# Pooled attention and a token/channel MLP on one core: scalings ahead of loads, heads that meet V sooner, and copies shared out anew

## The chip, the core and the metric

The kernel runs on one core of a Trainium2 chip. A core has five engines that work side by side, each with its own instruction stream: TensorE for matmuls (PE in the profile; its weight loads are listed as PEld), VectorE (DVE), ScalarE (ACT), GpSimd (POOL) and SyncE (SP), which here only issues transfers. POOL and ACT issue transfers too; the transfers themselves (DMA) run on the core's 16 DMA engines. [...] The metric is the device time of one execution in microseconds (us), as a median over runs.

## The reference

For each of 8 batches: attention with 8 heads of 64 columns over 576 tokens, with K and V averaged over groups of 8 tokens (72 groups), and behind it one block of a ResMLP, which mixes tokens and then channels. Cut to what matters:

```
k_p = k.reshape(B, H, 72, 8, D).mean(axis=3)
v_p = v.reshape(B, H, 72, 8, D).mean(axis=3)
scores = q @ k_p.T / sqrt(64)
attn = softmax(scores)
x = (attn @ v_p)                      # heads side by side: (B, 576, 512)
a1 = alpha1 * x + beta1
tok = einsum('ts,bsd->btd', w_tok, a1)
u = x + lam * tok
a2 = alpha2 * u + beta2
ch = relu(a2 @ w_ch1) @ w_ch2         # 512 -> 2048 -> 512
out = u + lam * ch
```

## The kernel before, in words

Matmul operands are in bf16 or f16, sums in f32. The batches are gone through in order. Attention of a batch gives x_tm, its x with the tokens in the partitions (4 chunks of 128, and a rest of 64 that two batches share a chunk for); the token mix turns it into u; u is transposed, and the MLP works on blocks of 4 such chunks (512 tokens). While PE does the MLP of one block it also does the attention and the mix of the next batch in between, and the order of all this is written by hand; no scheduler decides anything. The steps of one batch, as the change touches them:

- `att_F` (L591) transposes q on PE, L598 copies it out. `scores` and `scores_rest` (L707, L726 in the first batch; `att_S4`, L759 and L764, later) are the matmuls of q with the pooled K. ACT takes their exponentials (L712, L731, later L780) into ET.
- `first_V` (L685, copied out by L687) pools V for the first batch on PE. Later batches sum V on DVE: `att_V` (L697) adds halves of the 8 tokens of a group three times; the last one writes vp, the pooled V of four heads.
- `att_AV` (L798, L802) multiplies ET of one head with vp. A column of ones in vp gives the sum of the exponentials too. Then DVE takes its reciprocal (L805) and writes the product into x_tm (L807).
- `att_X` (L821) and `rest_X` (L814) scale x_tm of two or more heads by lam times alpha1 into xs, on POOL or DVE. The vector lam times alpha1 is spread over the partitions at the start in two halves by `spread_lamal` (PE L496, copied by L499).
- `mix_T` does the token mix (L887, w_tok transposed against xs), adds x_tm (L894, u_sb) and casts the sum to bf16 (L898, u_bf). In the first batch it goes by two column halves, one with heads 0 to 3 and one with heads 4 to 7. The 65th row of the weights holds row sums (`setup_rowsum`, L529 and L532), for beta1.
- `mix_uT` transposes u_bf. In the first block PE does it (L912), and the copy out of PSUM (L919 on ACT, four chunks of 128x128; or L922 on DVE, one instruction of 128x512) multiplies by alpha2.
- `mlp_A` is the first channel matmul (L944) with L952 (ACT, relu and bias, into H); `mlp_B` is the second (L965). In the first block a call of `mlp_A` does half the tokens and an extra column that gives the bias (L948).

The first batch has almost nothing to lie beside, and its order is the string `order` in the function at the end. Each word names a generator in `plan`, and each mention of a word runs that generator to its next `yield`; so the first `A2` is PE's matmuls of head 2 and the second is the reciprocal and the product on DVE. The letters: A is `att_AV` of a head, X and R are `att_X` and `rest_X`, F the q transposes, Q and P scores and exponentials, V `first_V`, s `spread_lamal`, W and r the transposes of w_tok (L516, copied by L520) and row sums, M `mix_T`, T `mix_uT`, H and G the two token halves of `mlp_A`. Loads stand in the same string: k0 and k1 (L301) are the two halves of K of the next batch, l1 to l4 the weights of the MLP (L557, L563), va and vb V of the next batch (L308). All of these are issued by POOL, in the order of the string and among POOL's own work; lr (L321) is issued by SP.

For later batches `attention(b)` makes a list of steps, each with a due time, and they are sorted by it and put among the matmuls of the MLP. A due time sets only the place in each engine's stream.

Of the kernel before, what the change touches and what calls it, by code (L numbers as in the profile page):

```python
# [10 lines left out]
AF = mybir.ActivationFunctionType  # L11
ALU = mybir.AluOpType
AX = mybir.AxisListType

P = 128
# [195 lines left out]
def kernel(  # L211
# [18 lines left out]
    nc = tc.nc  # L230
# [11 lines left out]
    def gp(name):  # L242
        if pair[0]:
            return psB.tile([P, 512], FP, tag="ch", bufs=2, name=name)
        return psA.tile([P, 512], FP, tag="gp", name=name)

    def whole(parts):
        for _ in parts:
            pass
# [150 lines left out]
    early = const.tile([P, 2, DM], F16, tag="early", name="early")  # L400
# [90 lines left out]
    def spread_lamal(half, copy):  # L491

        ps = gp("ps_bc")[:, 0:256]
        cols = slice(256 * half, 256 * half + 256)
        for c in range(2):
            nc.tensor.matmul(out=ps[:, 128 * c:128 * c + 128], lhsT=pick[:, 2 * half + c],  # L496
                             rhs=part)
        yield
        copy(out=lamal_bc[:, cols], in_=ps)  # L499
# [50 lines left out]
    al2_cols = const.tile([P, 4], FP, tag="al2_cols", name="al2_cols")  # L550
# [127 lines left out]
    def first_V(u, copy):  # L678

        ps_v = gp("ps_v")  # L680
        vp = ps_v[0:SPG, 0:4 * D]
        heads = slice(4 * u, 4 * u + 4)
        terms = [(identity_bf[0:SPG, 0:SPG], st1[0]["v16"][:, heads, c]) for c in range(8)]
        for i, (weights, t) in enumerate(terms):
            nc.tensor.matmul(out=vp, lhsT=weights, rhs=t, start=(i == 0), stop=(i == len(terms) - 1))  # L685
        yield
        copy(out=vp1_pool[u][:, :, 0:64], in_=vp.rearrange("p (h d) -> p h d", h=4))  # L687
# [212 lines left out]
    def mix_uT(key, copy=None):  # L900
        s = st2[key]
        i = where[key]
        blk, at = i // 4, i % 4
        if blk not in u_fm:
            u_fm[blk] = work.tile([P, 4, 512], BF, tag="u_fm", bufs=3, name="u_fm")
        if blk:
            nc.sync.dma_start_transpose(out=u_fm[blk][:, :, 128 * at:128 * at + 128],
                                        in_=s["u_bf"])
            return
        ps_uT = gp("ps_uT").bitcast(BF)  # L910
        for cc in range(4):
            nc.tensor.transpose(out=ps_uT[0:P, 128 * cc:128 * cc + 128],  # L912
                                in_=s["u_bf"][:, 128 * cc:128 * cc + 128], identity=identity_bf)
        yield
        o = u_fm[blk][:, :, at // 2, 128 * (at % 2):128 * (at % 2) + 128]
        i = ps_uT[:, 0:512].rearrange("p (c t) -> p c t", t=128)
        if copy is scalar:
            for cc in range(4):
                nc.scalar.activation(out=o[:, cc], in_=i[:, cc], func=AF.Copy, bias=0.0,  # L919
                                     scale=al2_cols[:, cc:cc + 1])  # L920
        else:
            nc.vector.tensor_tensor(out=o, in0=i, in1=al2_cols.unsqueeze(2).to_broadcast((P, 4, P)),  # L922
                                    op=ALU.mult)


    H4 = {}
# [292 lines left out]
    vector, scalar = nc.vector.tensor_copy, nc.scalar.copy  # L1219
# [18 lines left out]
        plan[f"K{u}"] = att_K(0, u, copy)  # L1238
    for u, copy in enumerate((vector, vector)):
        plan[f"V{u}"] = first_V(u, copy)  # L1240
    for u, copy in enumerate((vector, scalar)):
        plan[f"s{u}"] = spread_lamal(u, copy)
    for i, copy in enumerate((scalar, vector, scalar, vector)):
        plan[f"F{i}"], plan[f"P{i}"] = att_F(0, i, copy), scores(i)
# [5 lines left out]
        plan[f"R{h}"] = once(lambda h=h, n=n, eng=eng: rest_X(0, h, h + n, eng))  # L1250
    for c, copy in enumerate((vector, scalar, scalar, scalar, scalar)):
        plan[f"W{c}"] = setup_wtok(c, copy)
    for c, copies in enumerate(((scalar, scalar), (scalar, vector), (vector, vector), (vector, scalar))):
        plan[f"r{c}"] = setup_rowsum(c)
        plan[f"M{c}"], plan[f"T{c}"] = mix_T(0, c, copies[0]), mix_uT((0, c), copies[1])
        plan[f"H{c}"], plan[f"G{c}"] = mlp_A(0, c, 0, 256), mlp_A(0, c, 256, 512)
    in_pair = "A0 A3 F2 K0 M1 P1 T1 T3 W0 r0 r1 s0 s1".split()
    order = (
# [6 lines left out]
    for name in order.split():  # L1265
# [5 lines left out]
    def attention(b):  # L1271


        first = b == 1
        todo = []
        if first:
            for hp in range(4):
                todo.append((2.6 + 0.9 * hp, lambda hp=hp: whole(att_F(b, hp))))
            todo.append((3.5, lambda: cast_rem(b, nc.gpsimd, behind=nc.vector)))
            for u in range(2):  # L1280
                todo.append((3.65 + 0.1 * u, lambda u=u: load_w2(2 + u)))
            todo.append((7.4, lambda: whole(att_Frem(b, nc.scalar.copy))))
        if b < B - 1:
            at = 28.5 if first else 10.0
            todo.append((at, lambda: whole(att_F(b + 1, 0))))
            todo.append((at + 0.1, lambda: whole(att_F(b + 1, 2))))
            todo.append((19.3 if first else 23.1, lambda: cast_rem(
                b + 1, nc.gpsimd, behind=None if first else nc.vector)))
            todo.append((26.72 if b > 1 else 27.2, lambda: whole(att_Frem(b + 1))))
        for u in range(2):  # L1290
            if first:
                todo.append((3.6 + 0.1 * u, lambda u=u: sum_k(b, u, nc.gpsimd)))
            if b > 1:
                on_act = u == 0 or b == 3
                todo.append((2.5 + 2.0 * u if on_act else 8.55, lambda u=u, on_act=on_act:
                             add_rest(b, u, nc.scalar.copy if on_act else None)))
            if 1 < b < B - 1:
                todo.append((26.5 + 0.1 * u, lambda u=u: sum_k(b + 1, u, nc.gpsimd)))
                todo.append((26.73 + 0.1 * u, lambda u=u: turn_k(b + 1, u)))
            if b > 2:  # L1300
                todo.append(((4.1, 8.95)[u], lambda u=u: pool_k(b, u)))
                continue
            if first:
                todo.append((19.1 + 0.1 * u, lambda u=u: sum_k(2, u, nc.gpsimd)))
            todo.append((7.0 + 2.3 * u if first else 2.9 + 2.0 * u,
                         lambda u=u: whole(
                             att_K(b, u, nc.vector.tensor_copy if first else nc.scalar.copy))))
        for u in range(2):
            at = (9.0 if first else 6.3, 14.05 if first else 13.6)[u]
            todo.append((at, lambda u=u: att_S4(b, u)))  # L1310
            for k, dt in enumerate((0.1, 0.1, 0.1, 0.7, 1.7, 1.75) if u else ((0.1, 0.1, 0.1, 1.1, 2.1, 2.95) if first else (0.1, 0.1, 0.95, 1.0, 2.1, 3.1))):
                todo.append((at + dt, lambda u=u, k=k: st1[b]["exp", u](k)))
            early = (5.2, 5.7, 3.7, 4.2) if first else (5.7, 6.2, 2.9, 3.6)
            for i, dt in enumerate((2.9, 3.4, 4.6, 5.1) if u else early):
                h = 4 * u + i
                todo.append((at + dt, lambda h=h: whole(att_AV(b, h))))
                if i % 2:
                    eng = nc.gpsimd if h == 5 or first and h < 5 else nc.vector
                    todo.append((at + dt + 0.1, lambda h=h, eng=eng: att_X(b, h - 1, h + 1, eng)))
        for u in range(2):  # L1320
            when = (0.2, 1.4, 2.2), (12.7, 12.8, 13.0) if b == 2 else (5.0, 7.2, 8.0)
            if first:
                when = (10.6, 10.7, 10.8), (12.5, 14.3, 14.4)
            for i, at in enumerate(when[u]):
                todo.append((at, lambda u=u, i=i: att_V(b, u, 4 >> i)))
        for c in range(5):
            at = 22.0 + 1.1 * c if first else 21.0 + (1.3 if b == 2 else 1.15) * c
            if c < 4 or b % 2:
                todo.append((at, lambda c=c: whole(mix_T(b, c))))
                key = (b, c) if c < 4 else (b - 1, 4)  # L1330
                todo.append((at + 1.8, lambda key=key: whole(mix_uT(key))))
        return todo
# [22 lines left out]
    for n in range(NBLK):  # L1355
# [42 lines left out]
        if n >= FIRST:  # L1398
            when = ((3, (4.6, 14.6)), (1, (8.6, 18.91)), (2, (13.0, 18.92)), (4, (22.3, 23.0)))
# [20 lines left out]
        b = n + 1  # L1420
# [54 lines left out]
```

## Time and profile before

| | us |
|---|---|
| median of 3 runs | 325.3 (325.09 to 325.63) |
| the profiled execution | 325.52 |
| its span in the profile | 323.8 |
| PE busy | 314.9 |
| DVE busy | 264.3 |
| ACT busy | 181.5 |
| POOL busy | 133.8 |

The difference of 1.7 us between the execution and its span lies outside what the profiler records. TensorE's granted clock was 0.999 of full speed. In the profile, a row of a timeline has a start, a duration, the engine, the line, the operation, output and input, and how many instructions the row takes together; in brackets, the idle time before it and what the profile takes for its releaser. Matmuls overlap each other, and their ends are modelled, so the next one often starts before the row's end. The chain is the sequence of work that ended last, each piece with its start and duration.

### The profile page before, as it was taken

How to read it: one execution, taken by the hardware profiler on the slowest of the kernel's cores; microseconds unless marked ns; L12 is line 12 of the kernel's file. 1: busy time of each engine (PE TensorE's matmuls, PEld its weight loads, DVE VectorE, ACT ScalarE, POOL GpSimd, SP SyncE). 2: the span in 40 equal slices, each digit the busy share in tenths (PEclk: the TensorE clock that was granted, in tenths of full speed). 3: DMA queues.
4: the chain of work that ended last, by engine and by line, in shares of the span. 5: the costliest groups of instructions: out<-in, count | busy, mean ns of one | idle time of the engine just before them, and what ended most of it. 6: DMA issues, size and time to landing. Idle time of an engine off the chain costs nothing.

```text
span 323.8 us, 6638 instructions
## 1 busy us (share of the span) xinstructions
PE 314.9 (97%) x2476; PEld 212.5 (66%) x2500; DVE 264.3 (82%) x553; ACT 181.5 (56%) x364; POOL 133.8 (41%) x156
## 2 busy tenths in 40 slices
PE   7899999999999999999999999999999999999995
PEld 2688654455444576656775677558755868989984
DVE  6774686998689979797969797987788799989984
ACT  3876999278233951398129803792368335923930
POOL 8786465995256020800280027202520562611900
PEclk9999999999999999999999999999999999999999
DMA  7999999978896993499549964999560025004013
GB/s 195 204 226 260 212 193 260 151 204 143 167 254 101 226 159 101 90 275 163 161 93 222 185 180 82 179 214 153 139 180 2 0 51 162 2 1 131 3 34 97
DMA packets 73351, 47.41 MB, mean 146 GB/s; under 512 B 41282, under 2 KB 64098, under 8 KB 73318
## 3 DMA queue, kind: packets, MB, share of 16 engines
q1 hardware_dynamic: 59158, 34.65, 47.6%
q0 software_dynamic: 12896, 11.28, 21.5%
q10 hardware_dynamic: 1264, 1.05, 1.0%
q8 instruction: 19, 0.31, 0.4%
q14 instruction: 14, 0.11, 0.1%
HBM read 38.31 MB, written 9.44 MB: 147 GB/s over the span
## 4 chain that ended last, share of the span: by engine, by line
PE 91%; DVE 3%; DMA 2%; POOL 1%; issue 1%; ACT 1%; POOLq 0%; DVEq 0%; ACTq 0%
PE ps_h L944 31%; PE ps_w L1061 27%; PE ps_tok L887 12%; PE ps_ch L965 8%; PE ps_m L1134 6%; PE ps_av L798 3%; DMA q_bf<-in_q_dram 2%; PE ps_s L759 2%; PE ps_s L764 1%; PE ps_av L802 1%; DVE v_u L697 1%; ACT wtT L520 1%; PE ps_q L591 0%; DVE h_xs L1148 0%; POOL v L308 0%
## 5 line engine op out<-in xcount | busy, mean ns | idle before, releaser
L944 PE MATMUL ps_h<-u_fm,w 128*128 128x512 bf16 (+2 forms) x482 | 108.2, 366 | 1.1 <-DVE u_fm L922 0.4
L952 ACT ACTIVATE H<-ps_h,bias_cols 128x512 bf16<-128x512 f32 x116 | 78.4, 692 | 32.9 <-PE ps_h L944 31.7
L944 PEld LDWEIGHTS <-w 128*128 128x128 bf16 x496 | 53.0, 114 | 39.9 <-issue 2.0
L898 ACT CAST u_bf<-u_sb 128x512 bf16<-128x512 f32 x34 | 21.0, 619 | 73.9 <-issue 43.2
L1061 PEld LDWEIGHTS <-H 128*128 128x128 bf16 x560 | 53.4, 98 | 10.5 <-DVE u_sb L1079 0.8
L821 POOL TENSOR_TENSOR xs<-x_tm,lamal_bc 128x512 bf16<-128x512 f32 x12 | 15.2, 1270 | 101.1 <-DVE x_tm L807 100.7
L1061 PE MATMUL ps_w<-w,H 128*128 128x256 bf16 x448 | 53.6, 273 | 0.0
L1079 DVE TENSOR_TENSOR u_sb<-u_sb,ps_w 128x512 f32<-128x512 f32 x54 | 36.1, 683 | 11.5 <-PE ps_w L1061 10.9
L887 PE MATMUL ps_tok<-xs,wtT 128*128 128x512 bf16 (+5 forms) x214 | 44.8, 360 | 0.5
L780 ACT ACTIVATE ET<-ps_s 72x320 f16<-72x320 f32 (+1 forms) x84 | 37.1, 491 | 0.0
L807 DVE TENSOR_TENSOR x_tm<-ps_av,recs 128x320 f32<-128x320 f32 x64 | 31.4, 491 | 2.8
L894 DVE TENSOR_TENSOR u_sb<-x_tm,ps_tok 128x512 f32<-128x512 f32 (+1 forms) x40 | 27.2, 682 | 8.0 <-PE ps_tok L887 7.9
L965 PE MATMUL ps_ch<-w,H 128*128 128x512 bf16 x124 | 30.2, 379 | 0.2
L887 PEld LDWEIGHTS <-wtT 128*128 128x128 bf16 (+3 forms) x220 | 19.3, 100 | 15.2 <-issue 1.1
L697 DVE TENSOR_TENSOR v_u<-v_u 72x1024 f32<-72x1024 f32 (+1 forms) x24 | 24.2, 1007 | 0.4
L805 DVE RECIPROCAL recs<-ps_av 128x5 f32<-128x5 f32 x64 | 12.1, 189 | 13.2 <-PE ps_av L802 12.7
L1061 PE MATMUL ps_w<-w_t,h_s 128*128 128x256 bf16 x168 | 22.6, 272 | 0.0
L965 PEld LDWEIGHTS <-H 128*128 128x128 bf16 x128 | 11.9, 97 | 13.7 <-issue 0.4
L360 POOL TENSOR_TENSOR k_raw<-k_raw 128x512 f32<-128x512 f32 x14 | 19.2, 1371 | 3.8 <-DMA k_raw<-in_k_dram 3.8
L362 POOL TENSOR_TENSOR k_bf<-k_raw 128x512 bf16<-128x512 f32 x14 | 18.8, 1341 | 1.1
L1061 PEld LDWEIGHTS <-h_s 128*128 128x128 bf16 x168 | 16.4, 98 | 4.2
L798 PEld LDWEIGHTS <-ET 72*128 72x128 f16 x256 | 13.9, 97 | 6.4 <-issue 1.3
(189 smaller groups left out, 466.9 us busy)
## 6 DMA issues: line engine op xcount, KB each, us to landing
out_dram<-u_sb SPq DMA_DIRECT2D x29, 256.0 KB, 4.1
k_raw<-in_k_dram SPq DMA_DIRECT2D x13, 512.0 KB, 4.8
v_u<-in_v_dram SPq DMA_DIRECT2D x12, 512.0 KB, 6.0
q_bf<-in_q_dram POOLq DMA_DIRECT2D x15, 256.0 KB, 5.7
w<-in_moe_w_ch_dram POOLq DMA_DIRECT2D x6, 512.0 KB, 13.8
out_dram<-u_sb SPq DMA_DIRECT2D x10, 128.0 KB, 2.4
v<-in_v_dram POOLq DMA_DIRECT2D x4, 288.0 KB, 10.4
w<-in_moe_w_ch_dram POOLq DMA_DIRECT2D x1, 1024.0 KB, 14.1
```

Of the source, the lines that this page charges most:

```text
L697: nc.vector.tensor_tensor(out=out, in0=source[:, :, 0:width], in1=source[:, :, width:2 * width], op=ALU.add)
L780: nc.scalar.activation(out=o, in_=i, func=AF.Exp, bias=0.0, scale=0.125 if b < 3 else 0.125 * 0.125)
L798: nc.tensor.matmul(out=av[:, odd + c, :], lhsT=ET[:, m0:m0 + 128], rhs=vp1[:, h % 4, :])
L807: nc.vector.tensor_tensor(out=x[:, 1 - odd:6 - odd, dd:dd + D], in0=av[:, :, 0:64], in1=rec.unsqueeze(2).to_broadcast((P, 5, D)), op=ALU.mult)
L887: nc.tensor.matmul(out=ps_tok[p0:p1, cols], lhsT=wtT[0:kk, at, P * c:P * c + p1 - p0], rhs=xs_pool[i][0:kk, sc, cols], start=(sc == 0), st ...
L894: nc.vector.tensor_tensor(out=s["u"][p0:p1, :], in0=x[p0:p1, 1 + c if c < 4 else 5 - 5 * i, :], in1=ps_tok[p0:p1, 0:DM], op=ALU.add)
L898: copy(out=s["u_bf"], in_=s["u"])
L944: nc.tensor.matmul(out=ps_h[:, t0:t1 + one], lhsT=w1_of(cc, j), rhs=rhs, start=(cc == 0), stop=(cc == 3))
L952: nc.scalar.activation(out=H4[n, j // 4][:, j % 4, :], in_=ps_h, func=AF.Relu, bias=bias_cols[:, j:j + 1], scale=1.0)
L965: nc.tensor.matmul(out=ps, lhsT=H_of(n, j)[:, 128 * m:128 * m + 128], rhs=w2[j // 4][:, j % 4, :], start=(j == 0), stop=(j == NJ - 1))
L1061: nc.tensor.matmul(out=ps, lhsT=stat(j), rhs=moving(j), stop=(j == 7), start=(first and (pp == 0 or alone) and j == 0), skip_group_check=True)
L1079: nc.vector.tensor_tensor(out=o, in0=o, in1=banks[key, "both"], op=ALU.add)
```

## The change

The work is the same, and so is what is computed. Five things are placed otherwise:

1. `mix_uT` can share its copy between two engines: for "both", ACT scales chunks 2 and 3 (L919, two instructions) and DVE chunks 0 and 1 (L922, 128x256). T0 (before: ACT, four chunks) and T1 (before: DVE, 128x512) use it. The cast of M3's sum (L898) goes from DVE to ACT.
2. The copy of the second half of `spread_lamal` (L499) goes from ACT to DVE, and its matmuls come later in the string.
3. In `order`, the matmuls of heads 2, 3 and 0 come sooner: A2 and A3 ahead of the transposes F3 and F2. The scalings X2, X0 and R0 come sooner too, and the loads k0 and k1 are issued behind X6 instead of ahead of X2.
4. In `attention(1)`, head 1's product with V is due 0.4 later, which puts it behind another four matmuls of L944, and the second half's V sums are due sooner, which puts the last two of them on DVE ahead of the reciprocals and products of heads 0 and 1.
5. In `attention(2)`, the V sums of the second half are due sooner, which puts all three of them on DVE ahead of the scaling of heads 0 and 1 (L821, L814).

```diff
--- before.py
+++ after.py
@@ -914,13 +914,13 @@
         yield
         o = u_fm[blk][:, :, at // 2, 128 * (at % 2):128 * (at % 2) + 128]
         i = ps_uT[:, 0:512].rearrange("p (c t) -> p c t", t=128)
-        if copy is scalar:
-            for cc in range(4):
-                nc.scalar.activation(out=o[:, cc], in_=i[:, cc], func=AF.Copy, bias=0.0,
-                                     scale=al2_cols[:, cc:cc + 1])
-        else:
-            nc.vector.tensor_tensor(out=o, in0=i, in1=al2_cols.unsqueeze(2).to_broadcast((P, 4, P)),
-                                    op=ALU.mult)
+        n = {"both": 2, scalar: 0}.get(copy, 4)
+        for cc in range(n, 4):
+            nc.scalar.activation(out=o[:, cc], in_=i[:, cc], func=AF.Copy, bias=0.0,
+                                 scale=al2_cols[:, cc:cc + 1])
+        if n:
+            nc.vector.tensor_tensor(out=o[:, 0:n], in0=i[:, 0:n], op=ALU.mult,
+                                    in1=al2_cols[:, 0:n].unsqueeze(2).to_broadcast((P, n, P)))
 
 
     H4 = {}
@@ -1238,7 +1238,7 @@
         plan[f"K{u}"] = att_K(0, u, copy)
     for u, copy in enumerate((vector, vector)):
         plan[f"V{u}"] = first_V(u, copy)
-    for u, copy in enumerate((vector, scalar)):
+    for u, copy in enumerate((vector, vector)):
         plan[f"s{u}"] = spread_lamal(u, copy)
     for i, copy in enumerate((scalar, vector, scalar, vector)):
         plan[f"F{i}"], plan[f"P{i}"] = att_F(0, i, copy), scores(i)
@@ -1250,16 +1250,17 @@
         plan[f"R{h}"] = once(lambda h=h, n=n, eng=eng: rest_X(0, h, h + n, eng))
     for c, copy in enumerate((vector, scalar, scalar, scalar, scalar)):
         plan[f"W{c}"] = setup_wtok(c, copy)
-    for c, copies in enumerate(((scalar, scalar), (scalar, vector), (vector, vector), (vector, scalar))):
+    for c, copies in enumerate(((scalar, "both"), (scalar, "both"), (vector, vector), (scalar, scalar))):
         plan[f"r{c}"] = setup_rowsum(c)
         plan[f"M{c}"], plan[f"T{c}"] = mix_T(0, c, copies[0]), mix_uT((0, c), copies[1])
         plan[f"H{c}"], plan[f"G{c}"] = mlp_A(0, c, 0, 256), mlp_A(0, c, 256, 512)
     in_pair = "A0 A3 F2 K0 M1 P1 T1 T3 W0 r0 r1 s0 s1".split()
     order = (
         "ks wa l0 dr K0 c0 c1 F1 dq K0 F1 vm F0 d1 Fr P1 q0 V0 F0 Fr Q0 P0 P1 P1 q1 s0 Q0 P0 "
-        "K1 V0 Q0 F3 P0 s0 F2 K1 F3 A2 s1 A1 b0 A2 F2 s1 P3 P2 A3 A1 V1 P3 k0 Q1 A0 k1 A3 P3 "
-        "P2 ve Q1 V1 A0 W0 P2 W0 Q1 W1 A6 A4 A7 X2 W1 ve R0 A5 r0 A6 r0 X0 r1 A7 W4 A4 lr W2 "
-        "r1 A5 W4 W3 X4 M1 W2 W3 X6 l1 va l2 vb r2 M0 R6 r3 R4 M0 r2 r3 M1 M0 M3 M1 M0 M3 T0 "
+        "K1 V0 Q0 P0 A2 A3 F3 s0 F2 K1 A2 F3 A1 b0 A3 F2 P3 P2 A0 s1 A1 X2 V1 P3 Q1 A0 P3 P2 ve "
+        "Q1 V1 X0 s1 R0 W0 P2 W0 Q1 W1 A6 A4 A7 W1 ve A5 r0 A6 r0 r1 A7 W4 A4 lr W2 r1 A5 W4 W3 "
+        "X4 M1 W2 W3 X6 k0 k1 l1 va l2 vb r2 "
+        "M0 R6 r3 R4 M0 r2 r3 M1 M0 M3 M1 M0 M3 T0 "
         "M3 M1 M2 T0 T1 M2 T1 M3 H0 M2 M2 T3 H3 H0 T2 T3 H3 T2 H2 H2 H1 l3 l4 G3 G3 G0 G2 H1 "
         "G0 b1 G1 G1 G2")
     for name in order.split():
@@ -1310,7 +1311,7 @@
             todo.append((at, lambda u=u: att_S4(b, u)))
             for k, dt in enumerate((0.1, 0.1, 0.1, 0.7, 1.7, 1.75) if u else ((0.1, 0.1, 0.1, 1.1, 2.1, 2.95) if first else (0.1, 0.1, 0.95, 1.0, 2.1, 3.1))):
                 todo.append((at + dt, lambda u=u, k=k: st1[b]["exp", u](k)))
-            early = (5.2, 5.7, 3.7, 4.2) if first else (5.7, 6.2, 2.9, 3.6)
+            early = (5.2, 6.1, 3.7, 4.2) if first else (5.7, 6.2, 2.9, 3.6)
             for i, dt in enumerate((2.9, 3.4, 4.6, 5.1) if u else early):
                 h = 4 * u + i
                 todo.append((at + dt, lambda h=h: whole(att_AV(b, h))))
@@ -1318,9 +1319,9 @@
                     eng = nc.gpsimd if h == 5 or first and h < 5 else nc.vector
                     todo.append((at + dt + 0.1, lambda h=h, eng=eng: att_X(b, h - 1, h + 1, eng)))
         for u in range(2):
-            when = (0.2, 1.4, 2.2), (12.7, 12.8, 13.0) if b == 2 else (5.0, 7.2, 8.0)
+            when = (0.2, 1.4, 2.2), (12.51, 12.52, 12.53) if b == 2 else (5.0, 7.2, 8.0)
             if first:
-                when = (10.6, 10.7, 10.8), (12.5, 14.3, 14.4)
+                when = (10.6, 10.7, 10.8), (12.5, 13.9, 13.95)
             for i, at in enumerate(when[u]):
                 todo.append((at, lambda u=u, i=i: att_V(b, u, 4 >> i)))
         for c in range(5):
```

## The prediction

> **What bounds the kernel now.** I read the page's busy shares first, then the chain that ended last, then what PE waits for, and then, line by line, the stretches that the diff touches (12 to 36, 42 to 47 and 78 to 84 us).
>
> ```profile
> PE 314.9 (97%) x2476; PEld 212.5 (66%) x2500; DVE 264.3 (82%) x553; ACT 181.5 (56%) x364; POOL 133.8 (41%) x156
> ...
> PE 91%; DVE 3%; DMA 2%; POOL 1%; issue 1%; ACT 1%; POOLq 0%; DVEq 0%; ACTq 0%
> ...
> PE ps_q L591 <- DMA q_bf<-in_q_dram: 0.6, 1, 0.6
> PE ps_h L944 <- DVE u_fm L922: 0.4, 1, 0.4
> ...
> PE ps_av L798 <- DVE vp L697: 0.3, 1, 0.3
> ```
>
> PE is busy for 97% of the span and is 91% of the chain, and the diff adds and removes no matmul. So the time can change only by PE's waits, which are few: of the three shown, the first lies in the stretch that is reordered, and the other two are aimed at. Past 44 us PE follows a written order with hardly a gap, so what an early wait gives is kept to the end unless a later wait absorbs it.
>
> The chain through the first stage, start and duration:
>
> ```profile
> 18.34 1.64 ACT wtT L520 x3
> 19.98 0.12 issue
> 20.10 0.70 DVE xs L821
> ...
> 20.85 2.37 PE ps_tok L887 x20
> ```
>
> L821 is X4, the scaling of heads 4 and 5, and the second column half of the mix (L887 at 20.85) waits for it. The timelines of DVE and POOL about it:
>
> ```profile
> 20.10 0.69 DVE L821 TENSOR_TENSOR xs<-x_tm,lamal_bc 128x512 bf16<-128x512 f32 x1 [0.51 <-ACT wtT L520]
> ...
> 24.33 0.69 DVE L922 TENSOR_TENSOR u_fm<-ps_uT,al_cols 128x512 bf16<-128x512 bf16 x1 [0.38 <-PE ps_uT L912]
> ```
> ```profile
> 13.69 0.80 POOL L301 DMA_DIRECT2D k_raw<-in_k_dram  x1
> 14.65 0.75 POOL L301 DMA_DIRECT2D k_raw<-in_k_dram  x1 [0.16 <-DVE x_tm L807]
> 15.47 1.28 POOL L821 TENSOR_TENSOR xs<-x_tm,lamal_bc 128x512 bf16<-128x512 f32 x1
> ...
> 17.44 2.51 POOL L821 TENSOR_TENSOR xs<-x_tm,lamal_bc 128x512 bf16<-128x512 f32 x2
> 19.90 0.77 POOL L557 DMA_DIRECT2D w<-in_moe_w_ch_dram  x1
> ...
> 30.03 1.28 POOL L360 TENSOR_TENSOR k_raw<-k_raw 128x512 f32<-128x512 f32 x1
> ```
>
> X4 starts at 20.10, though its own input, the last product of L807, ended at 19.59 (19.10 + 0.49). Two things ended just before: ACT's W3 copy (19.97), which the view names, and POOL's X6 (19.95), which X4 does not read.
>
> PE's timeline about the wait at 82 us, and DVE's:
>
> ```profile
> 81.31 1.03 PE L965 MATMUL ps_ch<-w,H 128*128 128x512 bf16 x4
> 82.66 0.28 PE L798 MATMUL ps_av<-vp,ET 72*128 72x66 f16 x4 [0.32 <-DVE vp L697]
> ```
> ```profile
> 79.41 0.69 DVE L821 TENSOR_TENSOR xs<-x_tm,lamal_bc 128x512 bf16<-128x512 f32 x1
> 80.02 0.28 DVE L814 TENSOR_TENSOR xs<-x_tm,lamal_bc 64x128 bf16<-64x128 f32 x1
> 80.22 1.93 DVE L697 TENSOR_TENSOR v_u<-v_u 72x1024 f32<-72x1024 f32 x2
> 82.19 0.42 DVE L697 TENSOR_TENSOR vp<-v_u 72x256 f16<-72x256 f32 x1
> ```
>
> **The change part by part.** The sum is made against the profiled execution: 325.52 us, 0.22 over the median.
>
> *Attention meets V sooner; the second spread (L499) goes to DVE.* On PE, heads 2 and 3 now stand in the q_bf wait at 12.45. They need the exponentials that ACT ends at 12.30 (L712, 11.71 + 0.59), so two heads at 0.15 each (16.74, 16.89, 17.04) run at 12.35 and push the q transposes from 12.45 to about 12.65. Two later heads and the spread (L496, 13.15 to 13.36) leave their old places, and V1's transposes (L685) come at about 14.5 for 14.34: loss 0.16. On DVE the pair L805/L807 at 15.95 leaves (0.64 to the next start) and L499 comes in (0.42 there, 0.34 start to start). W0's copy, at 16.59, becomes free at 16.42, and A6's pair and what follows it up to A5's product come 0.17 sooner: 19.42 for 19.59. ACT loses 0.38 of L499 and W1 to W3 copies come some 0.07 sooner: 19.90.
>
> *X2, X0, R0 ahead of the k loads on POOL.* They no longer stand behind 1.6 us of issue, and X6 now waits for its input (A7's product, 18.32 - 0.17) and runs about 18.2 to 19.47. X4 can then start between 19.46 (its input) and 19.62 (X6's end and a hand-over as long as in the trace before, 0.15); I take 19.6, a gain of 0.5. It ends at 20.3. The mix's second half on PE also stands behind the row sums (L529 at 20.26 + 0.22, now 0.07 earlier), which ends at 20.47. So of the 0.5 a part is cut off: 20.85 becomes 20.48, gain 0.37. Bounds: 0.04 (X4 tied to ACT's W3) and 0.38.
> The row for X4 is 0.51 idle until POOL's X6 ended. [...]
>
> *T0 and T1 by "both".* ACT does 2 chunks of L919 (0.37 each, 0.26 start to start: 0.62), DVE 128x256 by L922. DVE's half is priced between 0.35 (half of 0.69) and 0.42 (the 128x256 casts); I take 0.42. In the built program DVE's half of each tile waits for ACT's last chunk of the same tile, so the halves follow each other. With everything 0.37 sooner: ACT ends T1's chunks at 24.51 (23.2 + 2 x 0.62, and a hand-over), DVE starts its half at 24.56 and ends at 24.98, for 25.02 before. L944 at 25.16 goes to 25.09. So 0.30 of the 0.37 is given back here. But DVE is also rid of M3's cast (L898 0.42, to ACT, free from 24.5 to 26.0), so M2's sum and cast end at about 26.04 for 26.41, and T2's transposes, which waited for the latter (26.47), come right behind PE's own work at about 26.2. The next L944 group stands behind T2's copy (26.90 + 0.69 = 27.59, then 27.65); this comes to 27.37. Gain of the first stage: 0.28, between -0.1 (the halves cost 0.1 more than I have) and 0.45.
>
> *k0, k1 behind X6 on POOL.* Issued at about 19.5 and 20.3 instead of 13.69 and 14.65; l1 (L557) moves from 19.90 to 21.0, va, l2 and vb by 0.6 to 1.1. From 24.15 on POOL's issues wait for loads of long before (24.15 and 26.35 name q_bf), so POOL is back in step there. The landings, issue and latency added, run on one after the other: q_bf 23.9 and 26.1, k0 27.5 (13.8 us behind its issue), k1 29.05 (14.4), l1 31.7 (11.8). k1 and l1 are issued 5.25 us apart and land 2.65 apart: the queue sets the landing and not the issue. An issue at 19.5 still stands before its turn at 26.1. I take nothing. Cover: k0 is first read at 30.03, 2.5 us behind its landing, and l1 by L572 on PE at 33.76, 2.06 behind. Bounds: 0 and 3.1 (below).
>
> *attention(1), 43 to 46 us.* Head 1's product moves behind the L944 group. Before, PE lost 0.07 ahead of 43.64, 0.17 ahead of 43.96 (ACT's exponential) and 0.14 ahead of head 4 at 45.82 (vp of L697 ends at 45.77). After: L944 at 43.64, head 1 at 44.50, L965 at 44.77 behind the exponential (44.72), head 4 at 44.77 + 4 x 0.216 = 45.63. vp is done by about 44.4, since its sum now fills DVE's 0.88 idle ahead of 43.77. Gain 0.19. POOL's L821 (42.97 to 44.23) now lies beside that sum; if the sum waits out the whole of it, vp is done at 45.4, still in time. Bounds 0 and 0.38.
>
> *attention(2), 82 us.* The L965 step is 0.216 (seven L944 from 79.80 to 81.31), so PE would be free at 81.31 + 4 x 0.216 = 82.175 and waited to 82.66: 0.48 (the view shows 0.32, since it counts modelled ends). The sums now start at 79.41 instead of 80.22, vp ends at 81.8, and no wait is left. Their data was requested at 51.16 on SP, so it is no bound. The displaced scaling (0.69 + 0.28) ends at 82.65, just as head 4's reciprocal becomes due. ACT's H and exponentials for the next L965 and heads end at 81.93 and 82.83, before PE comes to them (82.32 and 83.19). Gain 0.48, bounds 0.25 and 0.48.
>
> Sum: -0.28 - 0.19 - 0.48 = -0.95. 325.52 - 0.95 = 324.57 for an execution like the profiled one; with its 0.22 off, 324.35, say **324.4**.
>
> **The rivals.**
> *X4 is tied to ACT's W3*, as the view says. Then the mix is 0.04 sooner at most, and the halves that follow each other cost: ACT ends T1's chunks at 24.84, DVE its half at 25.31 instead of 25.02, and L944 and what stands behind it come 0.25 later. 0.25 - 0.19 - 0.48 = -0.42: 324.9. For it: the named releaser. Against: X4 reads nothing of W3, and DVE stretches beside POOL's scalings elsewhere too (the 72x512 sum of L697 took 0.84 at 44.47 beside POOL's L814, 0.69 at its shortest).
> *The gain at 82 us is absorbed later.* DVE does the same work behind it in another order; if a later product is as late as before, 0.48 is lost: 324.85. Against it: xs of these heads is first read by L887 at 87.6, five us after.
> *The halves run side by side.* Then T1 is ready 0.4 sooner, and the stage is bounded by T2 with 0.37: 324.25. Against it stands the built wait. [...]
> *Slower: k0 lands late.* If the landing follows the issue by 13.8 us, k0 lands at 33.3 instead of 27.5; POOL's L360 starts there and not at 30.03, k_bf is ready 3.27 later (32.72 + 3.27), and L668 on PE, at 33.13 and now 32.85, waits 3.1: -0.95 + 3.1, or 327.5. It decides from k0 landing at about 31.8: past 30.15 it costs one for one, and the gain is used up at 31.1. For it: 5.8 us of issue are lost. Against: the order of the landings above, and the page's latency for a load of k issued when less was queued, 6.2 us, which from 19.5 is 25.7.
>
> **How the numbers follow.** No change means within 0.2%, 0.65 us (324.65 to 325.95), about what this kernel's runs can tell. Forecast 0.49; X4 tied to W3 0.13 and absorbed 0.11, both no change; side by side 0.09, faster; slower 0.18, with other late waits of this kind in it. Faster 0.49 + 0.09 = 0.58, same 0.13 + 0.11 = 0.24, slower 0.18. The range leaves out the slower case: 323.9 (first stage 0.45, 43 us 0.38, 82 us 0.48, rounded down) to 325.3 (82 us absorbed, and the first stage at its loss of 0.1, rounded up).
>
> **What would show it.** X4 at 19.6 with POOL's X6 ending just before; L887 at 20.48; L944 at 25.09, its group behind T2 at 27.37; k landing still at 27 to 29 and L360 at 30.0; head 4 at 45.35 by the clock, with no vp wait there; no wait ahead of L798 at 81.2, and PE's order from there on 0.95 sooner. I am wrong if L668 near 32.9 waits for k_bf, if L944 at 25.1 comes later than before, or if the reordered first 14 us cost PE more than 0.16.

## The result and the profile after

| | before | changed |
|---|---|---|
| median of 21 runs, us | 325.26 (324.88 to 325.63) | 324.20 (324.02 to 326.27) |
| ratio, with its 95% interval | | 0.9978 (0.9968 to 0.9988) |
| span, median, us | 323.6 | 322.7 |
| time outside the span, median, us | 1.70 | 1.48 |

By the medians the change makes the kernel 1.06 us faster, 0.3% (324.20 / 325.26 = 0.9967). The ratio of the table is higher; it fits the means, which are 0.74 us apart and in which the long executions, told of next, weigh too. The forecast was 324.4. Of the 1.06 us some 0.9 lie in the span, and 0.2 outside it.

The changed kernel's profiled execution took 326.08 us, because TensorE's granted clock was 0.50 in it from 16.3 to 19.7 us, 3.4 us in all; three of its 21 executions show a low clock like this (means of 0.992 and 0.993). The table by stretch (length; busy time of PE, PEld, DVE, ACT, POOL; granted clock, DMA share, GB/s) has it in the second and third row:

```profile
14.00:16.00 2.00, 2.00 (x26) 1.32 (x21) 1.63 (x6) 1.56 (x3) 1.72 (x3) 1.00 1.12 210
16.00:18.00 2.00, 2.00 (x31) 1.98 (x30) 1.46 (x5) 1.67 (x7) 1.56 (x2) 0.58 1.13 211
18.00:20.00 2.00, 2.00 (x26) 1.72 (x24) 1.90 (x8) 0.86 (x6) 1.05 (x1) 0.57 1.14 207
```

At granted clocks of 0.58 and 0.57 PE does in these 4 us what takes about 2.3 at full clock, and what stands behind them comes some 1.5 us late in this one trace. The first stage is therefore read below from kernels that share its order and ran at full clock. The late part can be read here. PE's waits of the changed kernel:

```profile
PE ps_sc L707 <- DVE qT L598: 0.8, 2, 0.6
PE ps_h L944 <- DVE u_fm L922: 0.6, 1, 0.6
PE ps_kp L668 <- DVE k_bf L362: 0.4, 1, 0.4
PE ps_uT L912 <- DVE bias_cols L948: 0.2, 1, 0.2
```

The wait for vp (0.3 in the list of before) is gone from the list; the wait for u_fm is still there, and is longer. PE's timeline at 83 us, and DVE's:

```profile
82.66 1.03 PE L965 MATMUL ps_ch<-w,H 128*128 128x512 bf16 x4
83.52 0.28 PE L798 MATMUL ps_av<-vp,ET 72*128 72x66 f16 x4
...
83.67 1.03 PE L965 MATMUL ps_ch<-w,H 128*128 128x512 bf16 x4
```
```profile
80.64 1.94 DVE L697 TENSOR_TENSOR v_u<-v_u 72x1024 f32<-72x1024 f32 x2
82.61 0.42 DVE L697 TENSOR_TENSOR vp<-v_u 72x256 f16<-72x256 f32 x1
82.95 0.68 DVE L821 TENSOR_TENSOR xs<-x_tm,lamal_bc 128x512 bf16<-128x512 f32 x1
```

Head 4's L798 stands 0.86 behind the four L965, four steps of 0.216, so nothing waits; before, it stood 1.35 behind them.

### The profile page after: what moved, and what is told of

It is laid out like the page before. It is cut to its first block, busy times and chain, and to the rows that moved or that the text cites. A ratio compares the mean times of both kernels' runs of the same rounds, so it can differ in the third digit from the quotient of the medians.

```text
span 324.6 us, 6659 instructions
## 1 busy us (share of the span) xinstructions
PE 317.0 (98%) x2500; PEld 214.0 (66%) x2500; DVE 265.4 (82%) x554; ACT 181.7 (56%) x364; POOL 134.5 (41%) x156
## 4 chain that ended last, share of the span: by engine, by line
PE 94%; DVE 3%; DMA 2%; issue 0%; ACT 0%; DVEq 0%
PE ps_h L944 31%; PE ps_w L1061 27%; PE ps_tok L887 12%; PE ps_ch L965 9%; PE ps_m L1134 6%; PE ps_av L798 3%; PE ps_s L759 2%; DMA k_raw<-in_k_dram 2%; PE ps_s L764 1%; PE ps_w L516 1%; PE ps_v L685 1%; PE ps_av L802 1%; PE ps_rs L529 1%; DVE h_xs L1148 0%; PE ps_sc L707 0%; PE ps_kp L668 0%
## 5 line engine op out<-in xcount | busy, mean ns | idle before, releaser
L944 PE MATMUL ps_h<-u_fm,w 128*128 128x512 bf16 (+2 forms) x496 | 108.9, 366 | 0.6 <-DVE u_fm L922 0.6
L944 PEld LDWEIGHTS <-w 128*128 128x128 bf16 x496 | 53.1, 114 | 40.0 <-issue 2.1
L898 ACT CAST u_bf<-u_sb 128x512 bf16<-128x512 f32 x35 | 21.6, 619 | 73.2 <-issue 42.7
L821 POOL TENSOR_TENSOR xs<-x_tm,lamal_bc 128x512 bf16<-128x512 f32 x12 | 15.6, 1299 | 102.3 <-DVE x_tm L807 101.9
L887 PE MATMUL ps_tok<-xs,wtT 128*128 128x512 bf16 (+5 forms) x220 | 45.1, 361 | 0.0
L807 DVE TENSOR_TENSOR x_tm<-ps_av,recs 128x320 f32<-128x320 f32 x64 | 31.4, 491 | 2.8
L965 PE MATMUL ps_ch<-w,H 128*128 128x512 bf16 x128 | 30.5, 379 | 0.0
L887 PEld LDWEIGHTS <-wtT 128*128 128x128 bf16 (+3 forms) x220 | 19.3, 100 | 14.9 <-issue 1.1
L805 DVE RECIPROCAL recs<-ps_av 128x5 f32<-128x5 f32 x64 | 12.0, 188 | 11.6 <-PE ps_av L802 11.2
L965 PEld LDWEIGHTS <-H 128*128 128x128 bf16 x128 | 11.9, 98 | 13.5 <-issue 0.4
L360 POOL TENSOR_TENSOR k_raw<-k_raw 128x512 f32<-128x512 f32 x14 | 19.1, 1366 | 3.8 <-PE ps_tok L887 3.8
L798 PEld LDWEIGHTS <-ET 72*128 72x128 f16 x256 | 14.5, 100 | 5.7 <-issue 0.4
```

The costliest lines, as they stand in the source:

```text
L798: nc.tensor.matmul(out=av[:, odd + c, :], lhsT=ET[:, m0:m0 + 128], rhs=vp1[:, h % 4, :])
L807: nc.vector.tensor_tensor(out=x[:, 1 - odd:6 - odd, dd:dd + D], in0=av[:, :, 0:64], in1=rec.unsqueeze(2).to_broadcast((P, 5, D)), op=ALU.mult)
L887: nc.tensor.matmul(out=ps_tok[p0:p1, cols], lhsT=wtT[0:kk, at, P * c:P * c + p1 - p0], rhs=xs_pool[i][0:kk, sc, cols], start=(sc == 0), st ...
L898: copy(out=s["u_bf"], in_=s["u"])
L944: nc.tensor.matmul(out=ps_h[:, t0:t1 + one], lhsT=w1_of(cc, j), rhs=rhs, start=(cc == 0), stop=(cc == 3))
L965: nc.tensor.matmul(out=ps, lhsT=H_of(n, j)[:, 128 * m:128 * m + 128], rhs=w2[j // 4][:, j % 4, :], start=(j == 0), stop=(j == NJ - 1))
```

## The experiments

The times are medians, and what is read from a trace is one execution. Kernels timed together share the runs of before (325.25 to 325.31).

### The two halves of the change apart

Only the first stage (the diff without its last two hunks):

```diff
-            early = (5.2, 6.1, 3.7, 4.2) if first else (5.7, 6.2, 2.9, 3.6)
+            early = (5.2, 5.7, 3.7, 4.2) if first else (5.7, 6.2, 2.9, 3.6)
...
-            when = (0.2, 1.4, 2.2), (12.51, 12.52, 12.53) if b == 2 else (5.0, 7.2, 8.0)
+            when = (0.2, 1.4, 2.2), (12.7, 12.8, 13.0) if b == 2 else (5.0, 7.2, 8.0)
...
-                when = (10.6, 10.7, 10.8), (12.5, 13.9, 13.95)
+                when = (10.6, 10.7, 10.8), (12.5, 14.3, 14.4)
```

> Only the first stage of the change (parts 1 to 3); both attention steps are as before. By the prediction's sum the first stage gives 0.28 us: 325.0 against 325.3, head 4 at 82 us waiting for vp again (0.48). If X4 is tied to ACT's W3, it costs 0.25: 325.5. A second question: some executions of the changed kernel took about 1.9 us longer, and the profiled one of these shows PE at half rate from 16.2 to 19.4 us. If that comes from the new order of PE's work in the first 14 us, this kernel shows such executions too, near 327; if not, none.

And the same three lines changed in the kernel before, with its first stage as it was:

> Only the two attention steps (parts 4 and 5), the first stage as before. Prediction: 0.19 + 0.48 = 0.67 less, 324.6 against 325.3. If the gain at 82 us is absorbed later, 325.1; if the 43 us step gives nothing, 324.8. No long executions at all, if they come from the first stage's order; about as many as in the changed kernel, if they come from the chip's state at the time.

Measured: 324.99 with the first stage alone (ratio 0.9993, 0.9983 to 1.0004) and 324.54 with the attention steps alone (0.9980, 0.9971 to 0.9989), against 325.25. So 0.26 and 0.71 for forecasts of 0.28 and 0.67, and 0.97 in sum for 1.06. The interval of the first stage alone takes in no change at all. Its 0.26 is also not what was forecast: the span goes from 323.6 to 323.5 only, and the time outside the span from 1.71 to 1.48. The attention steps take the span from 323.6 to 322.9. One of 12 executions of the first took 326.62, and none of 11 of the second was long.

The attention steps alone, PE at 43 and 81 us:

```profile
43.28 0.30 PE L798 MATMUL ps_av<-vp,ET 72*128 72x66 f16 x4
...
43.52 1.03 PE L944 MATMUL ps_h<-u_fm,w 128*128 128x512 bf16 x4
44.38 0.28 PE L798 MATMUL ps_av<-vp,ET 72*128 72x66 f16 x4
...
44.65 1.02 PE L965 MATMUL ps_ch<-w,H 128*128 128x512 bf16 x4
45.51 0.28 PE L798 MATMUL ps_av<-vp,ET 72*128 72x66 f16 x4
...
81.00 1.03 PE L965 MATMUL ps_ch<-w,H 128*128 128x512 bf16 x4
81.86 0.29 PE L798 MATMUL ps_av<-vp,ET 72*128 72x66 f16 x4
```

Up to 43 us this trace runs 0.12 to 0.13 ahead of before's (43.28 for 43.41), by chance of the run. Head 4 at 45.51 instead of 45.82 is 0.31 ahead: the 43 us step gave 0.19. At 81.00 for 81.31 it is still 0.31, and head 4 of the next batch, 81.86 for 82.66, is 0.80 ahead: 0.49. Nothing in between takes anything back.

The same chance bears on the first stage, which is the same in these two kernels. The q transposes, which wait for the load of q_bf, come at 12.30 here and at 12.45 in the trace of before, and all that follows is 0.10 to 0.14 apart. So what the new order gives in the first stage is better read against this trace than against that of before. PE with the attention steps alone:

```profile
20.71 2.37 PE L887 MATMUL ps_tok<-xs,wtT 128*128 128x256 bf16 x20
...
25.03 0.60 PE L944 MATMUL ps_h<-u_fm,w 128*128 128x257 bf16 x4 [0.40 <-DVE u_fm L922]
...
33.02 0.28 PE L668 MATMUL ps_kp<-pool_main,k_bf 128*128 128x64 bf16 x4
```

With the first stage alone these three stand at 20.52, 25.05 and 32.92: 0.19 sooner, as late, and 0.10 sooner. The last is what is kept, and it fits the 0.1 in the span. PE and DVE with the first stage alone:

```profile
20.52 2.36 PE L887 MATMUL ps_tok<-xs,wtT 128*128 128x256 bf16 x20
```
```profile
18.91 0.49 DVE L807 TENSOR_TENSOR x_tm<-ps_av,recs 128x320 f32<-128x320 f32 x1
19.44 0.69 DVE L821 TENSOR_TENSOR xs<-x_tm,lamal_bc 128x512 bf16<-128x512 f32 x1
```

X4 starts 0.04 behind its input here, and 0.05 before POOL's X6 ends (19.49).

In the trace with the attention steps alone, DVE and POOL at 43 us show a row that the forecast had only as a bound:

```profile
42.69 0.68 DVE L697 TENSOR_TENSOR v_sums<-v_sums 72x512 f32<-72x512 f32 x1
43.40 1.38 DVE L697 TENSOR_TENSOR vp<-v_sums 72x256 f16<-72x256 f32 x1
```
```profile
42.85 1.64 POOL L821 TENSOR_TENSOR xs<-x_tm,lamal_bc 128x512 bf16<-128x512 f32 x1 [6.52 <-DVE x_tm L807]
```

vp takes 1.38 instead of 0.42, and POOL's L821 1.64 instead of some 1.28. DVE's first sum started before L821, which then ends 0.36 later than its 1.28 would have it; DVE's vp, which starts 0.55 behind L821, ends 0.3 behind it. vp is done at 44.78, 0.7 before head 4 needs it. By what means the two lengthen each other is not shown; L821 lost 0.36 where the sum ran 0.52 beside it.

### What held X4

The forecast laid X4's 0.51 idle on POOL's X6; the rival, with the view of before, on ACT's W3. First X6 alone was moved in the kernel before:

```diff
-        "r1 A5 W4 W3 X4 M1 W2 W3 X6 l1 va l2 vb r2 M0 R6 r3 R4 M0 r2 r3 M1 M0 M3 M1 M0 M3 T0 "
+        "r1 A5 W4 W3 X4 M1 W2 W3 l1 va X6 l2 vb r2 M0 R6 r3 R4 M0 r2 r3 M1 M0 M3 M1 M0 M3 T0 "
```

> The kernel before with POOL's X6 put behind the loads l1 and va, so that POOL works on no SBUF data between 18.7 and 20.2 us. If POOL's X6 held X4 on DVE, X4 starts at 19.6, right behind A5's product, while W3's copy on ACT still ends at 20.0. If W3 held it, X4 stays at 20.1. The time is longer, since the mix waits for X6 (to about 21.5).

Measured (one execution, 327.44): neither. DVE, and POOL beside it:

```profile
18.71 0.49 DVE L807 TENSOR_TENSOR x_tm<-ps_av,recs 128x320 f32<-128x320 f32 x1
19.71 1.29 DVE L821 TENSOR_TENSOR xs<-x_tm,lamal_bc 128x512 bf16<-128x512 f32 x1 [0.51 <-ACT wtT L520]
```
```profile
18.97 0.78 POOL L557 DMA_DIRECT2D w<-in_moe_w_ch_dram  x1
19.74 0.74 POOL L308 DMA_DIRECT2D v<-in_v_dram  x1
20.50 1.62 POOL L821 TENSOR_TENSOR xs<-x_tm,lamal_bc 128x512 bf16<-128x512 f32 x1
```

POOL scales nothing between 19.03 and 20.50, and W3's copy on ACT ends at 19.81, after X4's start. (X4 itself takes 1.29 here instead of 0.69, though X6 starts only 0.79 behind it; what stretched it is not shown.) Still X4 stands 0.51 behind its input, as in before and in the kernel with the attention steps alone. The view of line L821 in this kernel names one more instruction:

```profile
L821 DVEq EVENT_SEMAPHORE  x1: 21/21/21, 19.2 to 19.2; - x1
L821 DVE TENSOR_TENSOR xs<-x_tm,lamal_bc x1: 1292/1292/1292, 19.7 to 19.7; 128x512 bf16<-128x512 f32 x1
```

X4 has two waits: for A5's product on DVE, and for the copy of L499 on ACT, done over 5 us before. The program puts the first into an instruction of its own (EVENT_SEMAPHORE, at 19.2). In the trace of before it runs from 19.63 to 19.65, and X4 follows it 0.45 later, at 20.10. In the changed kernel L499 is on DVE, one wait is left, and that instruction is not there. So a new theory, and two kernels for it. The copy alone, in the kernel before:

```diff
-    for u, copy in enumerate((vector, scalar)):
+    for u, copy in enumerate((vector, vector)):
         plan[f"s{u}"] = spread_lamal(u, copy)
```

> The kernel before with one edit: the second copy of L499 on DVE instead of ACT. New theory: X4's 0.51 idle comes neither from POOL nor from ACT's W3, but from X4 having two waits, for A5's product (DVE) and for ACT's L499; the program puts the first into an instruction of its own, and X4 follows it by 0.45 whatever else runs. With L499 on DVE one wait is left: X4 starts 0.04 behind A5's product, though POOL's X6 still runs to about 19.95, L887's second half comes at 20.5, and the time is 0.2 to 0.3 less, 325.0. If POOL's X6 holds X4, X4 still starts near 20.0 and the time stays at 325.3.

And the changed kernel with this one line put back:

```diff
-    for u, copy in enumerate((vector, vector)):
+    for u, copy in enumerate((vector, scalar)):
         plan[f"s{u}"] = spread_lamal(u, copy)
```

> The changed kernel with only that copy of L499 put back on ACT. By the new theory X4 has its 0.51 idle again, though POOL's X6 is over by 19.5. DVE is rid of 0.34, so A5's product ends near 19.2, X4 starts near 19.7 instead of 19.45 and L887's second half comes at 20.5 to 20.6, within 0.1 of the changed kernel: the time stays at 324.2 to 324.3. If the order on POOL was what freed X4, X4 follows its product by 0.04.

Measured: 325.22 against 325.31 (0.9997, 0.9988 to 1.0006), and 324.61 (against 324.20 and 324.32 with the line). The first, DVE and POOL:

```profile
18.81 0.49 DVE L807 TENSOR_TENSOR x_tm<-ps_av,recs 128x320 f32<-128x320 f32 x1
19.33 1.06 DVE L821 TENSOR_TENSOR xs<-x_tm,lamal_bc 128x512 bf16<-128x512 f32 x1
```
```profile
17.33 2.51 POOL L821 TENSOR_TENSOR xs<-x_tm,lamal_bc 128x512 bf16<-128x512 f32 x2
```

The second, DVE (POOL's X6 ended at 20.19 here, another execution with the low clock, 0.993 in the mean):

```profile
19.54 0.49 DVE L807 TENSOR_TENSOR x_tm<-ps_av,recs 128x320 f32<-128x320 f32 x1
20.54 0.69 DVE L821 TENSOR_TENSOR xs<-x_tm,lamal_bc 128x512 bf16<-128x512 f32 x1 [0.51 <-ACT wtT L520]
```

With one wait X4 follows its product by 0.03 to 0.04; with two by 0.51, wherever POOL and ACT are. That part of the new theory holds. But with X6 still late on POOL (to 19.84) X4 takes 1.06 instead of 0.69 and ends 0.55 behind X6, so X6 bears on X4 too, behind the first obstacle, as a longer X4; by what means is not shown. Two kernels further down, in which X6 ends at 19.95 and 19.97 and X4 has one wait, show the same: X4 ends 0.56 and 0.55 behind X6. From the end of its input to its own end X4 takes 0.73 with neither obstacle (the first stage alone, 19.40 to 20.13), 1.09 with X6 alone, 1.20 with the second wait alone, and 1.20 with both (before, 19.59 to 20.79): one alone costs nearly as much as the two. That fits the copy alone, which gave 0.09 where 0.2 to 0.3 was expected. The order on POOL and PE without the copy lost 0.3 to 0.4 of the changed kernel's gain where 0.1 was expected; of this the span has 0.15 to 0.3 (323.0 against 322.7 and 322.85), and 0.13 lies outside it. Why the extra instruction costs 0.45 is not shown: elsewhere in the trace of before an instruction that comes behind such a wait for DVE's own result mostly follows it by 0.04 to 0.05 (19 of 22).

### The two halves of a copy

The changed kernel with T0, T1 and M3's cast as before:

```diff
-    for c, copies in enumerate(((scalar, "both"), (scalar, "both"), (vector, vector), (scalar, scalar))):
+    for c, copies in enumerate(((scalar, scalar), (scalar, vector), (vector, vector), (vector, scalar))):
```

> The changed kernel with the copies of T0, T1 and M3's cast as before (T0 all on ACT, T1 all on DVE). If the halves only follow each other, as the prediction has it, the split costs more than it gives: L944 at 24.8 instead of 25.1 and the group behind T2 at 27.3 instead of 27.4, so 0.1 faster than the changed kernel, 324.1. If the halves do run side by side, or the freed DVE time counts for more, it is 0.1 to 0.3 slower, 324.3 to 324.5.

Measured: 324.29 (five executions) against 324.20. In its trace L944 comes at 24.69 and L668 at 32.82, in the first stage alone with "both" at 25.05 and 32.92. But this trace is 0.13 ahead before the split begins (T0's transposes, L912, at 22.59 and 22.72). So the split costs 0.23 at the first MLP step and nothing at L668, and in the time no difference can be told. The first stage alone, DVE and PE:

```profile
23.89 0.42 DVE L922 TENSOR_TENSOR u_fm<-ps_uT,al_cols 128x256 bf16<-128x256 bf16 x1 [0.28 <-PE ps_uT L912]
24.58 0.42 DVE L922 TENSOR_TENSOR u_fm<-ps_uT,al_cols 128x256 bf16<-128x256 bf16 x1 [0.26 <-ACT u_fm L919]
```
```profile
25.05 0.60 PE L944 MATMUL ps_h<-u_fm,w 128*128 128x257 bf16 x4 [0.62 <-DVE u_fm L922]
```

DVE's second half waits 0.26 for ACT's chunks, though both halves are ready in PSUM (where PE's ps_ tiles lie). To give the halves a tile each, two kernels were made. First one that takes away the wait that was seen to come next, L668's for k_bf; in it K's first sum stands ahead of the casts of the rest on POOL:

```diff
-                todo.append((3.6 + 0.1 * u, lambda u=u: sum_k(b, u, nc.gpsimd)))
+                todo.append(((3.45, 3.7)[u], lambda u=u: sum_k(b, u, nc.gpsimd)))
```

> The changed kernel with K's first sum (L360, L362 of the first half) ahead of the casts of the rest (L351, L354) on POOL. Theory: part of the first stage's gain is lost at 32.9 us, where L668 now waits for k_bf, and k_bf is late because L354, ahead of it on POOL, waits for the rest's load (29.4 to 29.6). Then L360 starts near 28.1, k_bf is done near 30.8, the wait of 0.11 to 0.14 goes, and the time is 0.1 less than the changed kernel's. If L668 waited for something else, no change.

And then the halves in two tiles on top:

```diff
-        ps_uT = gp("ps_uT").bitcast(BF)
+        n = {"both": 2, scalar: 0}.get(copy, 4)
+        tiles = [gp("ps_uT").bitcast(BF) for _ in range(2 if n == 2 else 1)]
         for cc in range(4):
-            nc.tensor.transpose(out=ps_uT[0:P, 128 * cc:128 * cc + 128],
+            nc.tensor.transpose(out=tiles[cc // 2 if n == 2 else 0][0:P, 128 * cc:128 * cc + 128],
...
-    in_pair = "A0 A3 F2 K0 M1 P1 T1 T3 W0 r0 r1 s0 s1".split()
+    in_pair = "A0 A3 F2 K0 M1 P1 T3 W0 r0 r1 s0 s1".split()
```

> As the last one, and besides each shared copy (T0, T1) has its two halves in two PSUM tiles, so that no wait stands between ACT's half and DVE's. Theory: the halves follow each other only since they share a tile; now both of T1 end near 24.3, L944 starts near 24.4 instead of 25.05, M2's sum and cast come sooner with DVE free, and L668 comes 0.2 to 0.4 sooner than in the last one. If something else orders the halves (or the bank's other users do), L944 stays at 25.0.

Measured: 324.27 with the early sum and 323.87 with the two tiles as well (0.9957, 0.9944 to 0.9969). With the early sum L360 starts at 27.99, and L668 stands right behind PE's own work. The wait is gone, but 0.05 below the changed kernel's 324.32 in the runs beside it is no more than they can tell. The first stage alone shows that wait, on POOL and on PE:

```profile
29.55 0.73 POOL L354 TENSOR_TENSOR rem_k<-rem_raw 128x256 bf16<-128x256 f32 x1 [1.12 <-DMA rem_raw<-in_k_dram]
30.24 1.27 POOL L360 TENSOR_TENSOR k_raw<-k_raw 128x512 f32<-128x512 f32 x1
31.59 1.27 POOL L362 TENSOR_TENSOR k_bf<-k_raw 128x512 bf16<-128x512 f32 x1
```
```profile
32.36 0.61 PE L944 MATMUL ps_h<-u_fm,w 128*128 128x257 bf16 x4
32.92 0.29 PE L668 MATMUL ps_kp<-pool_main,k_bf 128*128 128x64 bf16 x4
```

Four L944 take 0.45 here, so L668 could have come at 32.81; k_bf, done at 32.86, held it 0.11.

In the two-tile kernel's profiled execution the first loads came late (PE waited 2.2 us for rem_k near the start) and the whole stage stands some 1.6 us late. The kernel with two tiles further down (k loads early) has T0's transposes at 22.79, as the one with the early sum alone: L944 comes at 24.40 instead of 25.12, and L668 at 32.50 instead of 32.87. The halves are plainer in a last variant, with M3's cast back on DVE:

```diff
-    for c, copies in enumerate(((scalar, "both"), (scalar, "both"), (vector, vector), (scalar, scalar))):
+    for c, copies in enumerate(((scalar, "both"), (scalar, "both"), (vector, vector), (vector, scalar))):
```

> The kernel with the halves in two tiles and the early sum of K, and M3's cast (L898) back on DVE. Theory: the next wait there is PE's L912 of T3 (0.34), which waits for M3's cast on ACT, behind ACT's chunks of T1. On DVE the cast is done 0.3 sooner, but M2's sum and cast come 0.2 to 0.3 later, and T2's transposes wait instead: within 0.1 of the kernel with two tiles, 323.8 to 324.0.

Measured: 323.69 (five executions, 323.65 to 323.74; ratio 0.9953, 0.9939 to 0.9967), the fastest of all, and a little more than the 0.1 below two tiles that was expected. DVE and PE:

```profile
23.37 0.75 DVE L922 TENSOR_TENSOR u_fm<-ps_uT,al_cols 128x256 bf16<-128x256 bf16 x2
24.04 0.42 DVE L898 CAST u_bf<-u_sb 128x512 bf16<-128x512 f32 x1
```
```profile
24.17 0.60 PE L944 MATMUL ps_h<-u_fm,w 128*128 128x257 bf16 x4
24.61 0.38 PE L913 MATMUL ps_uT<-identity_bf,u_bf 128*128 128x128 bf16 x4
24.83 0.61 PE L944 MATMUL ps_h<-u_fm,w 128*128 128x257 bf16 x4
25.57 0.40 PE L913 MATMUL ps_uT<-identity_bf,u_bf 128*128 128x128 bf16 x4
```

Both of DVE's halves now run back to back (one row, x2), L944 comes at 24.17 instead of 25.05 (0.15 of it is this trace's lead at T0's transposes), 0.06 behind PE's work before it, and what waits next is T2's transposes (L913 at 25.57, some 0.29), for M2's cast.

### The place of the k loads

```diff
-        "K1 V0 Q0 P0 A2 A3 F3 s0 F2 K1 A2 F3 A1 b0 A3 F2 P3 P2 A0 s1 A1 X2 V1 P3 Q1 A0 P3 P2 ve "
+        "K1 V0 Q0 P0 A2 A3 F3 s0 F2 K1 A2 F3 A1 b0 A3 F2 P3 P2 A0 s1 A1 k0 k1 X2 V1 P3 Q1 A0 P3 P2 ve "
...
-        "X4 M1 W2 W3 X6 k0 k1 l1 va l2 vb r2 "
+        "X4 M1 W2 W3 X6 l1 va l2 vb r2 "
```

> The changed kernel with the loads k0 and k1 issued ahead of X2 on POOL, about where they stood before. POOL's scalings X2, X0, R0 come up to 1.5 us later, X6 hardly. If the queue sets the landing, K lands at 27 to 29 us in both, and L360 on POOL starts near 30. X6 and with it X4 move by 0.2 at most: time within 0.2 of the changed kernel. If the place of the issue sets the landing, K lands earlier here by some 5 us, which no one needs: no change either, but shown in the latency.

The profile's view of the tile k_raw in this kernel, and in the first stage alone, where the loads are issued at 19.4 and 20.2:

```profile
L301 POOL DMA_DIRECT2D k_raw<-in_k_dram x2: 754/773/792, 13.4 to 14.7; - x2
...
DMA to landing us min/median/max: 14.2/14.3/14.3
```
```profile
L301 POOL DMA_DIRECT2D k_raw<-in_k_dram x2: 764/778/792, 19.4 to 20.2; - x2
...
DMA to landing us min/median/max: 8.4/8.7/9.0
```

Issued 6 us apart, they land at 27.7 and 28.9 and at 27.8 and 29.2: the queue sets the landing. The time is 324.51, 0.2 to 0.3 above the changed kernel. The span hardly shows it (322.8, against 322.7 and 322.85); most lies outside the span, 1.64 us here. The same edit in the kernel with two tiles and the early sum of K:

> The same kernel with two tiles and the early sum (M3's cast on ACT), and k0, k1 issued ahead of X2 on POOL. Two things went with the late issue so far: the executions with PE at half rate (8 of 50 with k0, k1 behind X6, none of 21 with them early), and a time outside the span of 1.47 us instead of 1.66 to 1.71. If both hang on the place of these two issues: no long execution at half rate here, and 323.9 + 0.2 = 324.1. If not: 323.9.

Measured: 324.04 against 323.87, with the same span (322.4) and 1.67 outside it instead of 1.46, and no long execution among five. And the changed kernel once more:

> The changed kernel itself, once more, since its first profile shows an execution with PE at half rate from 16.2 to 19.4 us. In an ordinary one: H0 (L944) near 25.05, K0 (L668) near 32.9 waiting 0.1 for k_bf, no wait for vp at 82 us; median 324.2. If the long executions (326) belong to this order of PE's work, about 1 in 5 to 1 in 10 again; if they were chance, none.

Measured: 324.32 (0.9980, 0.9966 to 0.9993), three of 12 executions at 326.0 to 326.4, the profiled one among them, with the same low clock between 16 and 20 us (0.50 in the first two of them, 0.66 in the others).

## Why the prediction was right, point by point

- **82 us**, forecast 0.48: 0.49. The displaced scaling cost nothing, so the rival that this gain is absorbed later was wrong.
- **43 us**, forecast 0.19: 0.19. vp was done at 44.8 instead of the forecast's 44.4 (beside POOL's L821 it took 1.38 for 0.42), and still in time.
- **The first 14 us.** The forecast had heads 2 and 3 wait for exponentials that end at 12.30, and push the q transposes to 12.65. They ran from 11.73 on, and the transposes came at 12.06. PE then waited 0.56 for DVE's copy of them (L598 at 12.93, behind head 2's product), a wait that the forecast did not have. V1's transposes came at 14.42 for the forecast's 14.5, a fit by luck. Against the trace with the attention steps alone (14.20) that is a loss of 0.22 for the forecast's 0.16.
- **The k loads**, forecast 0: landing unmoved. The slower rival was wrong.
- **X4's start and size**: forecast 19.6 (bounds 19.46 and 19.62), measured 19.44, just below them; L887 at 20.52 for 20.48, since it stands behind the row sums (L529 at 20.47), as forecast. The step's reason was wrong. No run shows the hold that the forecast's 0.5 for X4 rests on, an X4 that starts only behind POOL's X6: with the copy of L499 alone X4 started at 19.33, while X6 ran to 19.84. X4 did not idle for X6 but for its second wait; beside X6 it was then longer, 1.06 for 0.69, and no later. The price came out because the change removes both: the copy's place on DVE, which the forecast had only as 0.34 of DVE's time, and X6's earlier run. The rival with ACT's W3 was wrong: X4 started before W3's end.
- **The halves**: forecast DVE's last half at 24.56, L944 at 25.09 and the next group at 27.37; measured 24.58, 25.05 and 27.33. The forecast had "both" give back nearly all that X4 gave, and so it was: L944 is no sooner than with the attention steps alone (25.03). With two tiles it comes sooner.
- **The first stage's sum**, forecast 0.28, was too large. By the clock it is 0.32 at 27.3 us (27.65 to 27.33), but 0.11 of that is the late trace of before (27.54 with the attention steps alone), and L668 takes back 0.11. What is left is 0.1, in the trace (33.02 to 32.92) and in the span. The forecast had k_bf ready at 32.72 and 0.13 to spare; L354 ahead of it waited for a load that came 0.2 later. L668 waiting for k_bf is one of the signs by which the forecast called itself wrong; it came true in this small size.
- **The sum**, 324.4 for 324.2, is in part luck. In the spans the gain is 0.9 for the forecast's 0.95, of which the attention steps alone give 0.7. The first stage gave less than forecast. The time outside the span, for which the forecast had no term, fell from 1.70 to 1.48, and this is most of the 0.26 that the first stage alone gave in the time.

## What to carry to other kernels

An idle stretch that ends when two other engines finish need not belong to either: see whether it has the same length in every trace, and how many waits the idle instruction has. Obstacles that stand in series are not found by removing one: of X4's 1.20 us from input to end, taking away both saved 0.47, the second wait alone 0.11, and X6 alone nothing. In this program a copy shared by two engines ran in parallel only when the halves lay in different PSUM tiles (DVE's second half 0.33 behind its first, for 0.69 in one tile); give each its own, and look at once for the next thing that is late. Before two traces are compared by the clock, see how far apart they stand where the programs are still the same; and set the gain in the time beside the gain in the span, for the two can differ.

## What the runs showed of the hardware

- X4 on DVE, with two waits, one of them put into an instruction of its own, started 0.51 us after its input instead of 0.03. The length was 0.51 in all four traces that have the pair (before, the attention steps alone, X6 late, L499 back on ACT), with POOL and ACT at different points; other such pairs, as L805 and L807, mostly follow by 0.04 (19 of 22 in the trace of before). What makes the difference stays open.
- TensorE's granted clock was 0.50 for 3.4 us, from 16.3 to 19.7 us, in the profiled execution of the changed kernel, and matmuls of 128 columns stand 0.107 apart there from 16.3 to 19.2 us instead of 0.056. 8 of 78 executions of the kernels that issue k0 and k1 behind X6 have a low clock like this (0.992 to 0.995 in the mean, 1.6 to 2.1 us longer each), and none of 38 of the variants that issue them early, nor of before. (One of the eight of 50 that an expectation counts, 325.89, kept its clock, 0.999.) What brings it on is not shown. PE's longest gap in the 10 us ahead was 0.6 us, about as long as in the trace of before. That the late issue does it is not shown either: only 15 of the 38 also have the new order of PE's work, and at 8 in 78 none in 15 has a chance of about one in five.
- The time outside the span was 1.46 to 1.49 us (medians) in all seven sets of executions with late k loads and L499 on DVE, 1.62 with late k loads and L499 on ACT, and 1.64 to 1.72 with early k loads, before included. No row of a profile shows what it is; 0.2 us of the gain is in it.
